# Denominators of two residue parities in one matmul, paired transposes and wider dummy matmuls in a fused attention and FFN kernel

## The chip, the cores and the metric

The kernel runs on one core of a Trainium2 chip. The metric is the device time of one execution in microseconds (us). The median of three runs of the kernel before is 296.57 us (296.5 to 296.87).

The core has five engines with queues of their own: TensorE (PE), VectorE (DVE), ScalarE (ACT), GpSimd (POOL) and SyncE (SP). PE loads one operand into its array (the weights; PEld in the profile) and streams the other past it, one column after another. An operand of at most 64 partitions and 64 columns occupies one quadrant of the 128 by 128 array, and matmuls in different quadrants can run side by side.

## The reference

Eight batches of eight heads with 576 tokens and a head dimension of 64. Heads 0 to 3 attend to the last 32 tokens, heads 4 to 7 to 32 tokens at a distance of four from one another (the dilated heads). The output feeds a two-layer FFN with a squared ReLU.

```python
scores = scale * np.matmul(q, k.transpose(0, 1, 3, 2))
rel = pos[:, None] - pos[None, :]
mask_plain = (rel >= 0) & (rel < 32)
mask_dil = (rel >= 0) & (rel < 32 * 4) & (rel % 4 == 0)
attn = np.exp(scores masked); attn = attn / sum(attn)
x = matmul(attn, v)  ->  [4608, 512]
out = np.maximum(x @ w_in, 0) ** 2 @ w_out        # 512 -> 2048 -> 512
```

## The kernel before, in words

**Layout.** Tokens are taken as m*4 + r: r is the residue (0 to 3), m runs to 144. A dilated head then needs only tokens of the same residue. With r = 2c + j, j is the parity of the residue and c its half. Heads go in pairs e: e = 0, 1 are plain, e = 2, 3 dilated; a pair's two sides lie in partitions 0 to 63 and 64 to 127.

**The order of work.** The kernel schedules itself: each engine runs its instructions in the order in which the program issues them. The FFN is a list of groups of matmuls (`ffn_groups`, lines 967 and 1014, with evictions at 980, 983 and 1020). After group number g come the codes of the g-th part of the string `PROGRAM`, and the steps that a list of due places gives (`natural_step`). Attention for batch 0 is done ahead of the FFN and in its first groups by `first_step`, for batch 1 by `batch1`, for batches 2 to 7 by `quadrants`.

**Dummy matmuls.** At the start, while the first loads are on the way, the code s34x151 runs `turn(34, 151)` (line 760): 34 matmuls of zeros with 151 columns each, into a bank that nobody reads. They begin when the zeros are set. The transposes of batch 0 (line 790) follow on PE as soon as their queries and keys have landed.

**Transposes of batch 1.** The code 1t0 transposes queries and keys of the first 64 residue rows of all heads (line 564), between two FFN groups. The plain heads lie in partitions 0 to 63 of the staging tiles, the dilated ones in partitions 64 to 127. For each operand and each of eight slots z (head pair and residue) there are two transposes of 64 by 64 for the plain pair, to the lower and to the upper half of a PSUM bank, and two for the dilated heads, again to the lower and the upper half. The list is sorted by operand and slot, so that four transposes in four quadrants follow one another. The code 1cq0a and three others copy the results out, on ACT (one) and DVE (three); the scores (1s0) come three groups later. The second part of batch 1 (1t1p, 1t1d) has 80 rows and its own transposes; its dilated ones already take two residues at a time, 80 by 128.

**Denominators.** In `quadrants`, the sums of the exponentials are matmuls against a matrix of ones, issued by `issue` (line 369) as the other quadrant matmuls are. `issue` picks the quadrant whose clock of columns is furthest behind. For a dilated pair, batch 2 sums two pieces of 80 columns for both halves c of one parity (160 columns a matmul); batches 3 to 7 use sums formed before (`shared`) and have pieces of 48, 32 and 48. Each is done for j = 0 and for j = 1. The exponentials of the two parities lie 448 columns apart in the tile `pt`; `turn_` tells that they are stored in the other order. In `batch1`, the code 1b0 does the same for the first part with 128 columns for each parity.

Of the kernel before, what the change touches and what calls it, by code (L numbers as in the profile page):

```python
# [12 lines left out]
RES = 4  # L13
# [6 lines left out]

PROGRAM = (
# [42 lines left out]
def kernel(  # L64
# [10 lines left out]
    P = nc.NUM_PARTITIONS  # L75
    B, H, S, D = q.shape
# [19 lines left out]
    XB = 2  # L96
# [277 lines left out]
    def quadrants(scs, pvs):  # L374
# [16 lines left out]
        for n, (b, e) in enumerate(pvs):  # L391
# [16 lines left out]
            for g, rows in enumerate(sides):  # L408
# [29 lines left out]
                            D_.append((dend if to is None else d4[:, :, to], one, blk(i)[:, :, ms], z))  # L438
                    D_.append((d4[:, :, 112:120], one, blk(7)[:, :, 16:24], 32))
                else:  # L440
                    for j in range(2):
                        y = 448 * (j ^ turn_)
                        both = w[:, y : y + 320].rearrange("p (c m) -> p c m", c=2)
                        for m0, m1, rhs in (
                            (0, 80, both[:, :, 0:80]),
                            (48, 128, both[:, :, 80:160]),
                        ) if b == XB else (
                            (0, 48, both[:, :, 0:48]),
                            (48, 80, shared[rows, e - NE // 2, j ^ turn_]),
                            (80, 128, both[:, :, 112:160]),  # L450
                        ):
                            D_.append((d4[:, j::2, m0:m1], one, rhs, 2 * (m1 - m0)))
                    for x in range(2):
                        ms = slice(48 * x, 48 * x + 80)
                        for j in range(2):
# [68 lines left out]
    def batch1(code: str):  # L524
# [14 lines left out]
        if what == "t":  # L539
            at = code[2:] or "pd"  # L540
            todo = []
            for dil in ([0, 1] if part == 0 else ["pd".index(at[0])]):
                for x, nm in enumerate("qk") if part == 0 or not dil else [("qk".index(at[1]), at[1])]:
                    t = staged(1, nm)
                    if part == 0 and x == 0 or part and not dil or dil and part:
                        pool, name = (ps_f, "pf") if part and not dil else (ps_a, "pa")
                        bank = pool.tile([P, 1024], bf16, name=name)
                    to = bank[:, 512 * x : 512 * x + 512] if part == 0 else bank[:, 0 : 2 * w]
                    two[nm, dil] = to = to.rearrange("p (z m) -> p z m", m=n)
                    for z in range(2 * RES):  # L550
                        if part and dil:
                            todo.append((z, x, to[:, z, :], t[0:n, 1, H // 2 + z // 2, P * (z % 2) : P * (z % 2) + P], 0))
                            continue
                        for hl, rows in enumerate(sides):
                            if not dil:
                                src = t[0:n, part, 2 * (z // RES) + hl, D * (z % RES) : D * (z % RES) + D]
                            else:
                                r = 2 * (z % 2) + hl
                                src = t[64 : 64 + n, 0, H // 2 + z // 2, D * r : D * r + D]
                            todo.append((x, z, to[rows, z, :], src, 64 * (dil and part == 0)))  # L560
            if part == 0:
                todo.sort(key=lambda x: x[:2])
            for _, _, to, src, y in todo:
# [53 lines left out]
        elif what == "b":  # L617
# [6 lines left out]
            for e in (2, 3, 0, 1):  # L624
# [10 lines left out]
                for g, rows in enumerate(sides):  # L635
                    cols, P_, D_ = sides[g ^ crossed(1, e)], [], []
                    one = ones[rows, rows]
                    if e >= NE // 2:
                        for j in range(2):
                            y = 2 * cut * j + cut * (e - NE // 2)  # L640
                            main = two["p"][rows, y : y + cut].rearrange("p (c m) -> p c m", c=2)
                            for blk, _, q0, q1 in far_blocks[part]:
                                to, y0, z = slice(q0 - m0, q1 - m0), 48 * blk, q1 - q0
                                vt = vds[1, 1][rows, e - NE // 2, blk] if part else vds[1][rows, e - NE // 2, 0]
                                for half in range(2):
                                    r = 2 * half + j
                                    P_.append((f"o{e}", o[cols, r, to], vt[:, D * r : D * r + D], main[:, half, y0 : y0 + z], z))
                                d, key = ds[j * part]
                                d = d[cols, :, to] if part else d[cols, j::2, to]
                                D_.append((key, d, one, main[:, :, y0 : y0 + z], 2 * z))  # L650
                    else:
                        y = 0
                        for i, _, q0, q1 in blocks(1, e, part):
                            z = RES * (q1 - q0)
                            to, rhs = slice(q0 - m0, q1 - m0), byr(two["n", e][rows, y : y + z])
                            P_.append((f"o{e}", o[cols, :, to], vbd[1][rows, e, i, rows], rhs, z))
                            D_.append((ds[0][1], ds[0][0][cols, :, to], one, rhs, z))
                            y += z
# [629 lines left out]
```

## Time and profile before

| | |
|---|---|
| median of three runs | 296.57 us |
| the profiled execution | 296.83 us |
| its span, first to last instruction | 294.9 us |
| PE busy | 287.0 us (97%), 3323 matmuls |
| ACT busy | 186.9 us (63%) |
| DVE busy | 155.0 us (53%) |
| POOL busy | 123.6 us (42%) |
| FFN matmuls, line 967 | 127.8 us busy, 697 |
| FFN matmuls, line 1014 | 126.1 us busy, 571 |
| stretch of the transposes 1t0 | 39.71 to 40.43 us |

Matmuls overlap in the array, and the length that a row gives for one reaches to its modelled end; how fast a stream runs is read from one start to the next. A row of the order of time merges instructions of one kind that follow closely: it gives the start of the first, the time to the end of the last, and their count. `64*64` in a PE row is the number of rows and columns of the array that the instruction uses, `64x80` the shape of what it streams. Some matmul records are missing from the trace, which shows as a gap of one matmul's length put down to "issue".

### The profile page before, as it was taken

To read this page: it belongs to the slowest core of one execution; us is meant where nothing else is said; L and a number is where in the kernel's file an instruction comes from. 1 tells how busy PE (TensorE), PEld (TensorE's weight loads), DVE (VectorE), ACT (ScalarE), POOL (GpSimd) and SP (SyncE) were. 2 spreads that over 40 slices of the span, in tenths; PEclk is the share of its full clock that TensorE was granted. 3 is DMA by queue.
4 is the path that set the end of the run, shared out by engine and by line. 5 is a ranking of instruction groups with operands and counts; after the bars stand their busy time and mean duration, and the time that the engine had idled before them with its cause. 6 is when DMAs were issued, how large, how long until landed. Compare 5 with 4: busy or idle time off the path is not lost.

```text
span 294.9 us, 8115 instructions
## 1 busy us (share of the span) xinstructions
PE 287.0 (97%) x3323; PEld 166.3 (56%) x3351; DVE 155.0 (53%) x452; ACT 186.9 (63%) x379; POOL 123.6 (42%) x208
## 2 busy tenths in 40 slices
PE   7899999999999999999999999999999999999995
PEld 6689646859555554555455545554554455445443
DVE  2676225656669656686659464947455244005400
ACT  6788636868767774988567657766776466126511
POOL 8685267676648949376672779000000000000000
PEclk9999999999999999999999999999999999999999
DMA  7999999999999999999999599012101200121022
GB/s 118 192 178 208 206 219 188 173 193 172 178 220 170 125 207 140 190 118 150 154 178 132 79 155 177 7 36 75 36 0 39 73 36 2 36 71 36 2 71 71
DMA packets 82996, 35.48 MB, mean 120 GB/s; under 512 B 52384, under 2 KB 78208, under 8 KB 82960
## 3 DMA queue, kind: packets, MB, share of 16 engines
q0 software_dynamic: 49056, 18.49, 55.7%
q1 hardware_dynamic: 33760, 16.38, 27.6%
q8 instruction: 26, 0.43, 0.6%
q10 hardware_dynamic: 144, 0.10, 0.1%
q14 instruction: 10, 0.08, 0.1%
HBM read 37.50 MB, written 9.44 MB: 159 GB/s over the span
## 4 chain that ended last, share of the span: by engine, by line
PE 93%; DMA 2%; issue 1%; ACT 1%; POOL 1%; DVE 1%; ACTq 0%; POOLq 0%
PE pf L967 42%; PE pf L1014 42%; DMA kb<-in_k_dram 2%; PE po L369 2%; PE pa L369 2%; PE pf L369 2%; PE pd L369 1%; PE pa L790 1%; ACT h2T L980 1%; POOL qb L173 0%; PE pa L564 0%; DVE xT L913 0%; PE pf L842 0%; ACT rec L903 0%; PE po L760 0%
## 5 line engine op out<-in xcount | busy, mean ns | idle before, releaser
L967 PE MATMUL pf<-xT,w_in 128*128 128x512 bf16 (+1 forms) x697 | 127.8, 340 | 0.8 <-DVE xT L913 0.4
L1014 PE MATMUL pf<-w_out_sb,h2T 128*128 128x512 bf16 (+2 forms) x571 | 126.1, 373 | 1.5 <-issue 0.6
L980 ACT ACTIVATE h2T<-pf 128x512 bf16<-128x512 f32 x144 | 84.5, 600 | 32.1 <-PE pf L967 31.8
L967 PEld LDWEIGHTS <-w_in 128*128 128x128 bf16 x704 | 77.9, 113 | 47.0 <-issue 0.6
L983 DVE TENSOR_TENSOR h2T<-h2T 128x512 bf16<-128x512 bf16 x144 | 60.4, 425 | 63.1 <-ACT h2T L980 60.8
L1014 PEld LDWEIGHTS <-h2T 128*128 128x128 bf16 x592 | 56.1, 98 | 63.9 <-issue 0.3
L323 POOL DMA_DIRECT2D vbd<-in_v_dram x80 | 43.5, 554 | 21.7 <-DMA kb<-in_k_dram 9.1
L1020 ACT COPY osb<-pf 128x512 f32<-128x512 f32 (+1 forms) x34 | 19.5, 575 | 52.0 <-PE pf L1014 51.9
L173 POOL DMA_DIRECT2D qb<-in_q_dram x19 | 13.7, 720 | 8.4 <-DMA xx<-qb 6.6
L709 ACT ACTIVATE rec<-rec 128x576 f32<-128x576 f32 x24 | 16.4, 683 | 0.7
L173 POOL DMA_DIRECT2D kb<-in_k_dram x19 | 13.3, 699 | 6.8 <-DMA w_in<-in_moe_w_in_dram 2.9
L195 POOL DMA_DIRECT2D vbd<-in_v_dram x16 | 10.9, 685 | 9.6 <-DMA qb<-in_q_dram 3.9
L726 ACT ACTIVATE pt<-pa 128x384 bf16<-128x384 f32 (+1 forms) x26 | 11.7, 498 | 4.7 <-DVE xT L716 3.8
L309 POOL DMA_DIRECT2D vd<-in_v_dram x20 | 12.2, 621 | 4.5 <-DMA vbd<-in_v_dram 4.5
L315 POOL DMA_DIRECT2D vbd<-in_v_dram x20 | 12.0, 617 | 2.9 <-DMA vbd<-in_v_dram 2.9
L712 DVE TENSOR_TENSOR xT<-pf,rec 128x512 bf16<-128x512 f32 x11 | 7.6, 692 | 10.4 <-ACT rec L709 10.4
L712 DVE TENSOR_TENSOR xT<-po,rec 128x512 bf16<-128x512 f32 x13 | 9.0, 691 | 6.5 <-ACT rec L709 6.3
L728 DVE TENSOR_TENSOR pt<-pt,mask_f 128x384 bf16<-128x384 bf16 x24 | 8.5, 356 | 6.2 <-ACT pt L726 6.1
L728 DVE TENSOR_TENSOR pt<-pt,mask_n 128x384 bf16<-128x384 bf16 (+1 forms) x20 | 7.2, 374 | 8.6 <-ACT pt L726 8.5
L337 DVE COPY qT<-xx 64x576 bf16<-64x576 bf16 (+1 forms) x30 | 10.4, 348 | 0.6
L369 PEld LDWEIGHTS <-vbd 64*64 64x64 bf16 x328 | 8.3, 107 | 4.2 <-issue 3.7
L726 ACT ACTIVATE pt<-pf 128x448 bf16<-128x448 f32 (+1 forms) x18 | 8.6, 519 | 1.0 <-PE pf L369 0.7
(157 smaller groups left out, 281.0 us busy)
## 6 DMA issues: line engine op xcount, KB each, us to landing
qb<-in_q_dram POOLq DMA_DIRECT2D x7, 320.0 KB, 7.7
kb<-in_k_dram POOLq DMA_DIRECT2D x7, 320.0 KB, 9.6
vd<-in_v_dram POOLq DMA_DIRECT2D x34, 64.0 KB, 5.6
w_out_sb<-in_moe_w_out_dram POOLq DMA_DIRECT2D x4, 512.0 KB, 12.2
out_dram<-osb SPq DMA_DIRECT2D x16, 128.0 KB, 5.0
qb<-in_q_dram POOLq DMA_DIRECT2D x6, 256.0 KB, 6.9
kb<-in_k_dram POOLq DMA_DIRECT2D x6, 256.0 KB, 7.9
out_dram<-osb SPq DMA_DIRECT2D x9, 160.0 KB, 3.1
```

What stands on the lines that cost most here:

```text
L173: nc.gpsimd.dma_start(t[p0 : p0 + n, part, h0:h1, :], src[b, h0:h1, t0 : t0 + RES * n, :].rearrange("h (p r) d -> p h (r d)", r=RES),)
L323: nc.gpsimd.dma_start(v_rows[b % 2][p0 + 16 * r : p0 + 16 * r + 16, e, :, :], v[b, 2 * e + hl, :, :].rearrange("(i m r) d -> r m i d", r=R ...
L369: nc.tensor.matmul(out, lhs, rhs, start=begin, stop=True, skip_group_check=True)
L709: nc.scalar.activation(rec[:, :], rec[:, :], ACT.Exp, scale=-1.0)
L712: nc.vector.tensor_tensor(out=tok[:, :, 16:M], in0=byr(o[:, :]), in1=byr(rec[:, 0:512]), op=ALU.mult)
L726: nc.scalar.activation(pt, sp[b, e][g][:, 0:n], ACT.Exp, scale=SCALE)
L728: nc.vector.tensor_tensor(out=pt, in0=pt, in1=mask, op=ALU.mult)
L967: nc.tensor.matmul(to, w_in_sb[piece][:, kt, c0 : c0 + 509 : 4], rhs, start=(kt == kts[0] and x == 0), stop=(kt == kts[-1] and x == per - ...
L980: nc.scalar.activation(hv, acc[u][:, :].rearrange("p (x n) -> p x n", x=per), ACT.Relu)
L983: nc.vector.tensor_tensor(out=hv, in0=hv, in1=hv, op=ALU.mult)
L1014: nc.tensor.matmul(cur[m][:, c0:c1], h2[:, f, P * m : P * m + P], w_out_sb[:, f, c0:c1], start=(f == 0), stop=(f == NF - 1),)
L1020: (nc.vector.tensor_copy if last and part == 1 or tk0 == 3 * NT // 2 else nc.scalar.copy)(osb[:, c0:c1], cur[m][:, c0:c1])
```

## The change

Three edits; nothing moves between engines, and no wait is written by hand. PE has 102 matmuls fewer.

1. The dummy matmuls at the start: 20 of 256 columns in place of 34 of 151.
2. The denominators of a dilated pair: one matmul for both parities, with twice the columns, in `quadrants` (batches 2 to 7) and in the first part of `batch1`. A step of -1 over the parity takes the place of the swapped offset where `turn_` is 1.
3. The dilated transposes of 1t0: one of 64 rows by 128 columns for two residues, in place of two of 64 by 64. The list is sorted as before; in the built order each slot issues two 64 by 64 transposes of the plain pair and then one of 64 by 128.

```diff
-    "... L1:v0dp s34x151 T00 ..."
+    "... L1:v0dp s20x256 T00 ..."
...
-                    for j in range(2):
-                        y = 448 * (j ^ turn_)
-                        both = w[:, y : y + 320].rearrange("p (c m) -> p c m", c=2)
-                        for m0, m1, rhs in (
-                            (0, 80, both[:, :, 0:80]),
-                            (48, 128, both[:, :, 80:160]),
-                        ) if b == XB else (
-                            (0, 48, both[:, :, 0:48]),
-                            (48, 80, shared[rows, e - NE // 2, j ^ turn_]),
-                            (80, 128, both[:, :, 112:160]),
-                        ):
-                            D_.append((d4[:, j::2, m0:m1], one, rhs, 2 * (m1 - m0)))
+                    both = w[:, :].rearrange("p (j y) -> p j y", j=2)[:, :: 1 - 2 * turn_, 0:320]
+                    both = both.rearrange("p j (c m) -> p j c m", c=2)
+                    for m0, m1, rhs in (
+                        (0, 80, both[:, :, :, 0:80]),
+                        (48, 128, both[:, :, :, 80:160]),
+                    ) if b == XB else (
+                        (0, 48, both[:, :, :, 0:48]),
+                        (48, 80, shared[rows, e - NE // 2, :: 1 - 2 * turn_]),
+                        (80, 128, both[:, :, :, 112:160]),
+                    ):
+                        to = d4[:, :, m0:m1].rearrange("p (c j) m -> p j c m", c=2)
+                        D_.append((to, one, rhs, RES * (m1 - m0)))
...
+                        if dil:
+                            todo.append((x, z, to[:, z, :], t[64 : 64 + n, 0, H // 2 + z // 2, P * (z % 2) : P * (z % 2) + P], 64))
+                            continue
                         for hl, rows in enumerate(sides):
-                            if not dil:
-                                src = t[0:n, part, 2 * (z // RES) + hl, D * (z % RES) : D * (z % RES) + D]
-                            else:
-                                r = 2 * (z % 2) + hl
-                                src = t[64 : 64 + n, 0, H // 2 + z // 2, D * r : D * r + D]
-                            todo.append((x, z, to[rows, z, :], src, 64 * (dil and part == 0)))
+                            src = t[0:n, part, 2 * (z // RES) + hl, D * (z % RES) : D * (z % RES) + D]
+                            todo.append((x, z, to[rows, z, :], src, 0))
...
-                                d, key = ds[j * part]
-                                d = d[cols, :, to] if part else d[cols, j::2, to]
-                                D_.append((key, d, one, main[:, :, y0 : y0 + z], 2 * z))
+                                if part:
+                                    d, key = ds[j]
+                                    D_.append((key, d[cols, :, to], one, main[:, :, y0 : y0 + z], 2 * z))
+                        if part == 0:
+                            both = two["p"][rows, 0 : 4 * cut].rearrange("p (j e c m) -> p j e c m", j=2, e=2, c=2)
+                            d = ds[0][0][cols, :, :].rearrange("p (c j) m -> p j c m", c=2)
+                            D_.append((ds[0][1], d, one, both[:, :, e - NE // 2, :, :], 2 * cut))
```

2 rows, old and new, of the table PROGRAM are left out of this document.

## The prediction, made before the result was known

> **What bounds the kernel now.** I read the page first (busy time, slices, chain), then TensorE's waits, then one stretch that holds the whole middle of the run, and at the end the order of time around each line that the diff touches. The page:
>
> ```profile
> span 294.9 us, 8115 instructions
> PE 287.0 (97%) x3323; PEld 166.3 (56%) x3351; DVE 155.0 (53%) x452; ACT 186.9 (63%) x379; POOL 123.6 (42%) x208
> PE 93%; DMA 2%; issue 1%; ACT 1%; POOL 1%; DVE 1%; ACTq 0%; POOLq 0%
> ```
>
> The first line is the span, the second the busy shares, the last the shares of the chain that ended last. TensorE (PE) is busy for 97% and carries 93% of the chain. What it waited for longest over the whole run (us, times, longest), and one window (its length, PE's busy time and matmuls, clock, DMA share, GB/s):
>
> ```profile
> PE po L760 <- DVE kbd L1038: 1.1, 1, 1.1
> PE pa L790 <- DMA kb<-in_k_dram: 1.0, 2, 0.5
> 24.00:290.00 266.00, 264.06 (x2906) 1.00 0.82 117
> ```
>
> Both waits belong to the start: the first dummy matmul, and the first batch's keys. From 24 to 290 us PE lacks 1.9 us of being busy throughout, at the full granted clock. So after the start there is no wait that could swallow extra work: what is added to PE's in-order stream there comes out at the end, one for one, and so does what is taken away.
>
> **The second batch's transposes.** This is the large term. The old stage, in order of time on PE (start, length to the end of the last one, line, output<-inputs, rows*columns of the array in use, moving shape, count):
>
> ```profile
> 39.71 0.45 PE L564 MATMUL pa<-mk,qb 64*64 64x64 bf16 x32
> 39.98 0.51 PE L564 MATMUL pa<-mk,kb 64*64 64x64 bf16 x32
> 40.43 0.39 PE L1014 MATMUL pf<-w_out_sb,h2T 128*128 128x512 bf16 x1
> ```
>
> All 64 have one form, 64*64. Plain heads read partitions 0 to 63, dilated ones 64 to 127, each writing the lower or the upper half of the output, so four run side by side: 32 in the 0.27 us from 39.71 to 39.98, or 0.034 us for a round of four. The stage, from its first start to the next FFN matmul, takes 0.72 us.
>
> The change makes of each two dilated transposes one that fills all 128 columns over 64 rows. The list is still sorted by operand and slot, and in the built order each slot now issues two 64*64 transposes of the plain heads and then one of 64*128, sixteen times. So the array's form changes 31 times inside the stage, where it never changed before. What such a change costs:
>
> ```profile
> 12.41 0.19 PE L896 MATMUL pf<-pt,ones 128*128 128x64 bf16 x1
> 12.53 0.25 PE L880 MATMUL po<-pt,vd 64*64 64x64 bf16 x4
> ...
> 46.79 0.20 PE L564 MATMUL pf<-mk,kb 80*64 80x80 bf16 x1
> 46.92 0.26 PE L369 MATMUL pa<-pt,vd 64*64 64x64 bf16 x8
> ...
> 11.67 0.21 PE L790 MATMUL pa<-mk,kb 80*64 80x80 bf16 x2
> 11.80 0.26 PE L880 MATMUL pf<-pt,vbd 128*128 128x96 bf16 x2
> ...
> 49.34 0.45 PE L564 MATMUL pa<-mk,qb 80*128 80x80 bf16 x8
> 49.62 0.28 PE L967 MATMUL pf<-xT,w_in 128*128 128x256 bf16 x1
> ...
> 10.42 0.20 PE L842 MATMUL pf<-xx 64*64 64x64 bf16 x2
> 10.55 0.39 PE L760 MATMUL po<-kbd 128*128 128x512 bf16 x1
> 10.87 0.22 PE L842 MATMUL pf<-xx 64*64 64x64 bf16 x2
> ...
> 229.50 6.64 PE pf L1014 x30
> ```
>
> In the stage above a 64-column round is followed after 0.03 us. Before a change of form the next matmul starts 0.12 us after one of 64 columns (first pair). The second pair changes only the rows (80 rows need all 128), the third only the columns: 0.13 us each for 80 columns. The fourth shows that the wait is not a matter of leaving transposes: 80*128 needs the same array as 128*128, and eight transposes and the next FFN matmul follow one another every 0.035 us. The next three rows show one matmul alone between two changes, as the stage would have: 0.13 us into it and 0.32 us out of it, against the 0.22 us of a 512-column step (last row, of the chain: 30 in 6.64 us).
>
> So a change costs about 0.09 to 0.10 us over the work, in both directions and for either dimension. The new stage has 32 stretches (16 pairs, whose two run side by side, and 16 singles), each followed by a change, the last by the one to the FFN. At 0.12 us for a stretch that is 3.84 us, at 0.14 (0.13, and the 0.01 more that the lone matmul showed) 4.48; I take the middle, 0.13: 4.16 us, against 0.72 before: 3.4 us more. If a change between two forms with disjoint rows costs nothing, the stage stays at 16 rounds of 0.034 us and about its 0.72: that is the other end, no gain of note, since the two halves were already running side by side.
>
> The pages of the Trainium skill bear on the one thing that no row shows, a change between 64*64 and 64*128. "TensorEngine Tiling (Array Packing)", section Tiling Modes, says that "Changing tiling mode (not just tile) drains the TensorE", and lists these two as different modes; the rows above agree for four other changes, and by that rule the term is the 3.4 us. The same section says that tiles operate independently, which by itself would give the zero.
>
> What stands behind the stage is not late for a second reason:
>
> ```profile
> 40.56 0.59 ACT L569 COPY xx<-pa 128x512 bf16<-128x512 bf16 x1 [0.16 <-PE pa L564]
> 42.12 0.41 DVE L571 COPY qT<-pa 128x512 bf16<-128x512 bf16 x1
> 43.12 0.32 PE L369 MATMUL pa<-xx 64*64 64x64 bf16 x16
> ```
>
> The copies out of the transposes' banks follow them by 0.16 us and end at 42.53; the scores that use them start at 43.12. Copies and scores shift together with PE, so this slack of 0.6 us stays. ACT's and DVE's evictions of later FFN groups are queued behind those copies, but their producers on PE shift as well. No DMA is moved past another; loads issued by POOL become early relative to PE.
>
> **The denominators.** For a dilated pair of batches 3 to 7 each half of the partitions issued 96, 64 and 96 columns twice; it now issues 192, 128 and 192. The columns are the same; what goes is what a matmul costs beside its columns. By group (count, busy us, mean ns, idle before) and in order of time:
>
> ```profile
> L369 PE MATMUL pd<-pt,ones 64*64 64x64 bf16 x28 | 5.2, 193 | 0.0
> L369 PE MATMUL pd<-pt,ones 64*64 64x128 bf16 x22 | 4.5, 218 | 0.0
> 52.94 0.21 PE L369 MATMUL pd<-qT,kbd 64*64 64x96 bf16 x2
> 53.12 0.19 PE L369 MATMUL pd<-qT,kbd 64*64 64x64 bf16 x2
> 47.07 0.28 PE L369 MATMUL pa<-pt,ones 64*64 64x128 bf16 x8
> ```
>
> In the first two rows 64 columns more cost 25 ns, so 0.4 ns each. Four rounds of 96 columns lie between 52.94 and 53.12, so one is 45 ns, of which some 39 are columns. A round of 64 is 34 ns; one of 128 is 60 (eight in two rounds: 0.28 less the 0.22 of one). Merging two of 96 saves about 4 ns, two of 64 about 8: some 15 ns for each pair and half. The halves use different quadrants and run at once, so 5 batches by 2 pairs give 0.15 us. In batch 2 (four 160-column pieces become two of 320) and in the second batch's first part (two of 128 become one of 256) the same 4 ns count five times: 0.02 us, inside the rounding. The ends: nothing, if another quadrant of the visit ends later; and 36 matmuls taken out of a row at a whole 34 ns each, 1.2 us. I take 0.15, since the columns stay. The new reads have one dimension more and for some halves run backwards over the parities; no row has a backward read, and I count it as nothing, from the 96-column rounds above, whose reads and writes are already split (24 by 4) and cost no more than their columns and those few ns.
>
> **The dummy matmuls.** 34 of 151 columns (5134) become 20 of 256 (5120).
>
> ```profile
> 1.07:4.01 2.94, 2.94 (x24) 1.00 0.65 109
> 4.12 0.76 PE L760 MATMUL po<-kbd 128*128 128x151 bf16 x9
> 4.52 0.36 PE L760 MATMUL po<-kbd 128*128 128x151 bf16 x3
> 4.81 0.31 PE L790 MATMUL pa<-mk,qb 64*64 64x64 bf16 x8
> 5.55 0.22 PE L790 MATMUL pa<-mk,kb 64*64 64x64 bf16 x2 [0.43 <-DMA kb<-in_k_dram]
> ```
>
> The first row is a window from the first of them to 4.01 us: 24 in 2.94 us, 0.122 us each. The next two are the last nine and the last three: six of them lie between 4.12 and 4.52, 0.067 each. The array runs at half speed first and at full speed from some 4 us on, which the granted clock does not show. With the same columns the new ones end where the old did. If the full speed came later they would run at 0.207 us each, to 5.2 us, and the first query transposes would still be done at about 5.5, when the keys land at 5.55. The 0.43 us wait for that DMA is the cover; cost 0.
>
> **The sum.** Profiled execution: 296.83 us around its span of 294.9; 3.4 - 0.15 makes it 300.1. It lies 0.26 over the median of the runs shown, 296.57, so the forecast is **299.9 us**, 299.5 to 300.2 by the 0.12 and 0.14 us.
>
> **The rivals.**
>
> *Disjoint rows need no stop* (not slower). The single transpose sits in rows 64 to 127, the pair in rows 0 to 63; if PE stops only where forms overlap, the stage stays at 0.72 us and the denominators' 0.15 remain: 296.4 us. Against it: every change among the rows above stops; for it: in all of them the rows overlap, so they cannot tell. It decides once a change costs under about 0.02 us. 12%.
>
> *Only one direction stops*, say into the wide form: 16 stretches of 0.13 us and 16 of 0.034 are 2.6 us, 1.9 more than before: 298.3 us. The rows show both directions stopping alike. 6%.
>
> *The array falls back to half speed.* For 4.2 us PE would stream 64 columns in every 0.13 us, about a fifth of its time. If that counts as idle, the following FFN runs like the first dummies, at 0.122 instead of 0.067 for a step; a slow stretch as long as that first one, 2.94 us, loses 2.94 x (1 - 0.067/0.122) = 1.3 us: 301.2 us. Against it: at the start PE twice waited 0.5 us for keys between small transposes, and the 512-column matmul at 10.55 us still took full-speed time. 8%. The Trainium skill ("TensorE: Matmul & The Clock Gate", Part 1) puts the fall behind an idle window of about 3.4 us, and its Part 4 has transposes not counting as busy; no run here shows either, and by its own window the loss would be an estimated 1.7 us.
>
> **How the numbers follow.** The forecast's own mechanism has 74%, the rivals 12, 6 and 8. The range is 298.0 to 301.2: it holds the forecast's mechanism, up to 0.17 us for a stretch (4.6 us net of 0.72), and the one-direction case, 80% together; the clock's fall starts at its upper edge. A difference of 0.2% (0.6 us) is about what can be told from no change. The no-stop rival at 296.4 is within it, unless the removed matmuls save toward their upper end: 0.10 for the same, 0.03 for faster. All the rest is slower: 0.87.
>
> **What would show it.** In the changed profile: 48 transposes at the stage's line, 16 of them 64*128, with starts about 0.13 us apart at each change, and the stage 4 us long instead of 0.72; FFN groups behind it shifted by 3.4 us, all else on PE equal but for shifts; visits with dilated denominators 15 ns shorter; the key transposes at the start unmoved at 5.55. If wide and narrow transposes start within 0.03 us of each other the forecast is wrong at its main step; a stage of 4 us with FFN steps of 0.4 us behind it is the clock.

## The result and the profile after

The changed kernel takes 306.98 us (median of six executions, 305.42 to 310.28) against 296.72 for the kernel before on the same chip (six, 296.44 to 299.25): a ratio of 1.0319 with a 95% interval of 1.0257 to 1.0381. It is slower, as forecast, but by 10.3 us where 3.3 were forecast, and lies above the range. The ratios, here and below, leave out executions whose clock was unusually low (here the one of 310.28 us; in a_narrow two, of 303.2 and 303.6), so they differ from the ratio of the medians. The profiled execution took 309.0 us, 12.2 more than the profiled execution of before. Its page (span, busy time, the granted clock in 40 slices, the shares of the chain):

```profile
span 307.1 us, 7911 instructions
PE 294.5 (96%) x3221; PEld 169.1 (55%) x3249; DVE 156.5 (51%) x452; ACT 187.3 (61%) x379; POOL 122.9 (40%) x208
PEclk9999997999799999999999999999999999999999
PE 85%; DMA 9%; POOL 3%; issue 1%; DVE 1%; ACT 0%; ACTq 0%; POOLq 0%
```

PE has 102 matmuls fewer and is busy for 7.5 us more. In two slices (of 7.7 us each) the granted clock is down, and the chain now runs 9% over DMAs, where it ran 2%. The waits of PE, by length (us, times, longest):

```profile
PE pa L369 <- DVE qT L278: 2.8, 1, 2.8
PE pf L845 <- issue: 1.2, 1, 1.2
...
PE pf L970 <- DMA w_in<-in_moe_w_in_dram: 0.7, 1, 0.7
...
PE pa L369 <- DMA xx<-qb: 0.6, 1, 0.6
```

None of these four was there before. The stage of the transposes, in order of time on PE (the first three rows are the stage as a whole; of the others, from narrow stretches inside it, each merges what follows it closely, so only its start and form are read):

```profile
41.33 2.30 PE L563 MATMUL pa<-mk,qb 64*64 64x64 bf16 x24
43.56 2.30 PE L563 MATMUL pa<-mk,kb 64*64 64x64 bf16 x24
45.79 0.61 PE L1017 MATMUL pf<-w_out_sb,h2T 128*128 128x512 bf16 x1
...
41.75 0.35 PE L563 MATMUL pa<-mk,qb 64*128 64x64 bf16 x3
41.88 0.35 PE L563 MATMUL pa<-mk,qb 64*64 64x64 bf16 x3
42.03 0.34 PE L563 MATMUL pa<-mk,qb 64*128 64x64 bf16 x3
```

The stage takes 4.46 us instead of 0.72. A wide transpose is followed after 0.13 us by a narrow pair, and that after 0.15 us by the next wide one: 16 times 0.28 us. Windows over the stage, the stretch behind it and a later one (us; PE busy, weight loads, DVE, ACT, POOL; granted clock, DMA share, GB/s):

```profile
41.33:45.79 4.46, 4.46 (x49) 3.18 (x49) 0.00 (x0) 0.58 (x1) 2.31 (x4) 1.00 1.36 215
45.79:49.20 3.41, 3.19 (x9) 1.21 (x10) 1.35 (x3) 0.58 (x1) 3.18 (x6) 0.50 1.14 145
79.90:83.30 3.40, 3.40 (x18) 2.44 (x17) 1.78 (x6) 2.24 (x6) 1.11 (x2) 0.51 1.57 192
```

Right behind the stage the clock is halved (0.50 of full speed) for 3.41 us, and once more at 79.9.

Both kernels issue the same instructions on ACT in the same order, so how far each of them is shifted says where the 12.2 us arise:

| place in the changed kernel | shift added, us |
|---|---|
| first batch's scores (PE out of instructions, 13.8 to 15.0) | 0.8 |
| up to 24.5 (PE waits for a load of w_in) | 0.9 |
| the stage of the transposes | 3.7 |
| half clock, 45.8 to 49.2 | 1.7 |
| third batch's scores (waits of 0.55 and 2.75) | 3.6 |
| half clock, 79.9 to 83.3 | 1.6 |
| the rest, to the end | -0.1 |

From 84 us on the shift stays at 12.1 to 12.2 us. So the longer stage itself is less than a third of it; the third batch's scores and the half clock behind them are more. Where these come from, the order of time on SP, POOL, DVE and PE shows; first of before:

```profile
51.89 1.43 SPq L254 DMA_TRANSPOSE xx<-kb  x1
56.18 1.25 SPq L254 DMA_TRANSPOSE xx<-qb  x1
...
56.88 0.74 POOL L173 DMA_DIRECT2D qb<-in_q_dram  x1
...
63.59 0.17 DVE L345 COPY kbd<-xx 64x128 bf16<-64x128 bf16 x1
```

and of after:

```profile
58.93 2.00 SPq L254 DMA_TRANSPOSE xx<-kb  x1
65.16 2.55 SPq L254 DMA_TRANSPOSE xx<-qb  x1
...
58.15 0.76 POOL L173 DMA_DIRECT2D qb<-in_q_dram  x1
...
75.58 0.27 DVE L345 COPY kbd<-xx 64x128 bf16<-64x128 bf16 x1 [4.87 <-DMA xx<-qb]
...
77.80 0.46 DVE L278 COPY qT<-pd 128x576 bf16<-128x576 bf16 x1
...
78.67 0.33 PE L369 MATMUL pa<-xx 64*64 64x80 bf16 x14 [2.75 <-DVE qT L278]
```

The third batch's dilated queries and keys reach their places by four transposing loads on SP's queue (line 254). Before, they were issued from 51.89 to 56.18, ahead of POOL's loads of the next queries and keys (line 173, from 56.88), and the last landed 6.4 us after its issue, 1.0 us before DVE came to them at 63.59 and found them there. Now SP's queue is 7 to 9 us later, since ahead of these loads stand stores of FFN results that wait for ACT and so for PE; POOL's queue is only 1.3 us later, at 58.15. The order of the two is turned round. The last transposing load lands 10.4 us after its issue, and DVE waits 4.87 us for it. Of these, 1.9 come from its being issued 9.0 us later where DVE is ready only 7.1 us later (70.71 against 63.59), 4.0 from the longer landing, less the 1.0 us of margin before. The copies queued behind it on DVE (line 278) are late with it, and PE waits 0.55 and 2.75 us.

### The profile page after: what moved, and what is told of

It reads as the page before. It is cut to its first block, busy times and chain, and to the rows that moved or that the text cites. A ratio compares the mean times of both kernels' runs of the same rounds, so it can differ in the third digit from the quotient of the medians.

```text
span 307.1 us, 7911 instructions
## 1 busy us (share of the span) xinstructions
PE 294.5 (96%) x3221; PEld 169.1 (55%) x3249; DVE 156.5 (51%) x452; ACT 187.3 (61%) x379; POOL 122.9 (40%) x208
## 4 chain that ended last, share of the span: by engine, by line
PE 85%; DMA 9%; POOL 3%; issue 1%; DVE 1%; ACT 0%; ACTq 0%; POOLq 0%
PE pf L970 39%; PE pf L1017 39%; DMA w_in<-in_moe_w_in_dram 5%; DMA xx<-qb 3%; PE po L369 2%; PE pa L563 2%; PE pa L369 1%; PE pf L369 1%; PE pd L369 1%; POOL vbd L195 1%; POOL qb L173 1%; POOL kb L173 1%; DVE kbd L348 0%; POOL vd L214 0%; DVE qT L278 0%
## 5 line engine op out<-in xcount | busy, mean ns | idle before, releaser
L970 PE MATMUL pf<-xT,w_in 128*128 128x512 bf16 (+1 forms) x697 | 129.7, 344 | 1.1 <-DMA w_in<-in_moe_w_in_dram 0.7
L1017 PE MATMUL pf<-w_out_sb,h2T 128*128 128x512 bf16 (+2 forms) x571 | 127.5, 376 | 1.7 <-issue 0.9
L173 POOL DMA_DIRECT2D qb<-in_q_dram x19 | 13.5, 713 | 18.2 <-DMA xx<-qb 15.6
L729 ACT ACTIVATE pt<-pa 128x384 bf16<-128x384 f32 (+1 forms) x26 | 11.7, 498 | 8.3 <-PE pa L369 4.5
L309 POOL DMA_DIRECT2D vd<-in_v_dram x20 | 12.2, 626 | 4.2 <-PE pa L369 3.2
L337 DVE COPY qT<-xx 64x576 bf16<-64x576 bf16 (+1 forms) x30 | 10.7, 357 | 0.6
L369 PE MATMUL pa<-xx 64*64 64x80 bf16 (+2 forms) x208 | 6.5, 198 | 3.3 <-DVE qT L278 2.8
## 6 DMA issues: line engine op xcount, KB each, us to landing
w_out_sb<-in_moe_w_out_dram POOLq DMA_DIRECT2D x4, 512.0 KB, 13.8
```

The lines of the kernel that those rows point to most:

```text
L173: nc.gpsimd.dma_start(t[p0 : p0 + n, part, h0:h1, :], src[b, h0:h1, t0 : t0 + RES * n, :].rearrange("h (p r) d -> p h (r d)", r=RES),)
L369: nc.tensor.matmul(out, lhs, rhs, start=begin, stop=True, skip_group_check=True)
L970: nc.tensor.matmul(to, w_in_sb[piece][:, kt, c0 : c0 + 509 : 4], rhs, start=(kt == kts[0] and x == 0), stop=(kt == kts[-1] and x == per - ...
L1017: nc.tensor.matmul(cur[m][:, c0:c1], h2[:, f, P * m : P * m + P], w_out_sb[:, f, c0:c1], start=(f == 0), stop=(f == NF - 1),)
```

## The experiments

After the result, three explanations stood beside the long stage. One: the lower clock follows from a stage that leaves the array thinly used; against it, that transposes as such do not count, or that the fall has nothing to do with the stage. Two: the wait for the transposing loads follows from any delay of PE ahead of them; against it, that the wide transposes themselves or the later clock bring it. Three: the wait at the start comes from the number of instructions in the dummies; against it, from their length.

**The two halves of the change (a_narrow, b_wide_only).** The first is the changed kernel with the old 64 narrow transposes; the second is the kernel before with the wide transposes alone.

```diff
 # a_narrow, against the changed kernel (b_wide_only: the reverse, in the kernel before)
-                        if dil:
-                            todo.append((x, z, to[:, z, :], t[64 : 64 + n, 0, ...], 64))
-                            continue
...
+                            if not dil:
+                                src = t[0:n, part, 2 * (z // RES) + hl, ...]
+                            else:
+                                r = 2 * (z % 2) + hl
+                                src = t[64 : 64 + n, 0, H // 2 + z // 2, D * r : D * r + D]
+                            todo.append((x, z, to[rows, z, :], src, 64 * (dil and part == 0)))
```

> The changed kernel with its transposes of the second batch put back to 64 by 64; dummies and denominators stay changed. Theory (the whole loss comes from the wide transposes and what follows them): 296.4 us, the stage of transposes 0.72 us, no stretch at half clock, visits with dilated denominators about 15 ns shorter. Rival (the dummies let the start run late, as the +0.5 to +1.7 us before the stage in the changed profile suggest, or the denominators' backward reads cost): 297.5 to 298.5 us, with the late first 25 us again in the profile.

> The kernel before with the wide transposes alone. Theory: the same as the changed kernel within its scatter, 305 to 308 us: a stage of 4.4 to 4.5 us, then 3.4 us at half clock, and a later wait for the third batch's scores of about 3 us. Rival (part of the loss belongs to the dummies): 302 to 304 us, without the lateness before the stage.

Measured: 298.8 us for a_narrow (1.0044, interval 1.0 to 1.0088), which is the rival's side, and 304.96 for b_wide_only (1.0283, 1.0238 to 1.0328), just below what was expected. Waits of PE in b_wide_only:

```profile
PE pa L369 <- DVE qT L278: 2.1, 1, 2.1
...
PE pf L841 <- issue: 0.2, 1, 0.2
```

The wide transposes alone bring a stage longer by 3.74 us, half clock for 3.4 us behind it (1.72 us lost) and the wait at the third batch's scores (2.3 us with what hangs on it). The rest of the change brings the wait for instructions at the start, 1.6 us in a_narrow against 0.2 here, and in the profiled execution neither of the other two.

**What the clock follows (c_grouped, f_split, k_dense, s_thin).** c_grouped keeps the wide transposes but does all narrow ones of an operand ahead of its wide ones, so that the form changes three times inside the stage instead of 31.

```diff
-                todo.sort(key=lambda x: x[:2])
+                todo.sort(key=lambda x: (x[0], x[4], x[1]))
```

> The changed kernel with the same wide transposes, sorted so that the plain ones of an operand come first and its eight wide ones after them: 3 changes of form inside the stage instead of 31. Theory (the changes of form cost, not the wide form): 32 rounds of 0.032 us and 4 changes of 0.1 us make a stage of about 1.45 us, 0.75 more than before; no half clock; 297.0 to 297.5 us. Rival (the wide transposes are slow by themselves, or by their weight loads): a stage of 3 us or more and 300 us or more.

Measured: 300.29 us (1.0117, 1.0051 to 1.0183), some 3 us above what was expected. In order of time, its stage:

```profile
40.09 0.78 PE L563 MATMUL pa<-mk,qb 64*64 64x64 bf16 x24
40.79 0.77 PE L563 MATMUL pa<-mk,kb 64*64 64x64 bf16 x24
41.50 1.25 PE L1017 MATMUL pf<-w_out_sb,h2T 128*128 128x512 bf16 x4
```

1.41 us instead of 4.46 with the same 48 transposes: it is the changes of form that cost, as was expected (1.45 us). No half clock follows. The time was missed through waits: 1.4 us for instructions at the start, and the one at the third batch's scores, which stays:

```profile
PE pa L369 <- DVE qT L278: 1.6, 1, 1.6
```

Here the transposing loads are issued only 1.1 to 1.7 us later than before (from 52.94 to 57.88), but POOL's at line 173 begin at 55.84, and the last transposing load landed 11.4 us after its issue. PE also ran out of instructions for 1.0 us at line 272, just ahead of this.

f_split keeps the 31 changes and takes the stage apart: the queries' transposes come two FFN groups earlier, the keys' at the old place.

```diff
-    "M11 | ... |  |  | 1t0 1cq0a 1ck0 1pk0 1pq0 |  |  | 1s0 1e0 1f0 |  | "
+    "M11 | ... | 1t0 |  | 1u0 1cq0a 1ck0 1pk0 1pq0 |  |  | 1s0 1e0 1f0 |  | "
```

> The changed kernel with the queries' half of the wide transposes two FFN groups earlier, so that about 1.7 us of FFN at full rate lies between the two halves; as many changes of form as before. Theory (the clock falls because TensorE streams little for more than a window of about 3.4 us): no stretch at half clock behind the stage, each half 2.2 us, together 3.8 us more than the old stage; 1.7 us better than the changed kernel, 303.5 to 305.5 us, the later wait included. Rival (the clock falls for another reason, the transposes or the changes of form themselves): a stretch at half clock again.

Measured: 307.87 us (1.0354, 1.0302 to 1.0407). Windows over both halves and behind them:

```profile
38.50:45.00 6.50, 6.50 (x53) 3.51 (x51) 0.00 (x0) 1.17 (x2) 4.15 (x7) 1.00 1.36 175
45.00:49.00 4.00, 4.00 (x47) 2.08 (x49) 1.35 (x3) 0.58 (x1) 2.71 (x5) 1.00 1.14 131
```

The two halves together cost 3.8 us, as the stage did, and in the profiled execution no half clock follows either of them: two stretches of 2.2 us with 1.8 us of FFN between them do not bring the fall there. Whether they would in another place is open (see the last section). The total gained nothing all the same, and missed the 303.5 to 305.5 us expected. This kernel had its half clock at 14.8 to 18.2 us instead, behind a wait for instructions at the start, and a wait of 2.5 and 1.4 us at the third batch's scores, with half clock from 76.2 to 83.1.

k_dense issues the 64 narrow transposes six times over in the kernel before, to have as long a stage without a change of form. The repeats write the same results again.

```diff
-            for _, _, to, src, y in todo:
+            for _, _, to, src, y in todo * (6 if part == 0 else 1):
```

> The kernel before with the second batch's 64 narrow transposes issued six times over, densely: a stage of about 3.3 to 3.7 us without changes of form (the first five passes are overwritten by the last, so nothing is left out). Theory (a thin stream lets the clock fall, not the transposes as such): no half clock behind it, 2.6 to 3.0 us more, plus up to 3 us at the third batch's scores. Rival (transposes do not count as work for the clock, however dense): 3.4 us at half clock behind the stage.

Measured: 315.36 us (1.0629, 1.059 to 1.0668). Its waits:

```profile
PE pa L564 <- issue: 8.3, 2, 5.1
```

PE ran out of instructions inside the stage, for 8.3 of its 13.3 us, so the stage was not dense. Half clock came too, but from 44.3 us on, inside the first of these waits. The run does not answer its question.

s_thin answers it from the other side: ahead of the narrow transposes of the kernel before it puts 32 matmuls of zeros with 64 columns, in turn 64*64 and 128*128. There is no transpose among them.

```diff
+            if part == 0:
+                spare = ps_o.tile([P, 512], f32, name="po")
+                for _ in range(16):
+                    for n_ in (64, P):
+                        nc.tensor.matmul(spare[0:n_, 0:64], idle[0:n_, 0:n_], idle[0:n_, 0:64], start=True, stop=True, ...)
```

> The kernel before with 16 pairs of small matmuls of zeros ahead of the second batch's transposes, 64 columns each, one over 64*64 and one over 128*128 in turn: 32 changes of form without a transpose; nothing is left out. Theory (a change costs 0.09 to 0.12 us whatever it stands beside, and a thin stream of 4 us lets the clock fall): a stretch of 4.1 to 4.6 us, then 3.4 us at half clock, then up to 4 us at the third batch's scores: 304 to 307 us. Rival (the clock falls because transposes do not count as work): no half clock behind it, 301 to 304 us.

Measured: 306.06 us (1.0298, 1.0247 to 1.0349). In order of time, and in windows:

```profile
39.00 4.92 PE L567 MATMUL po<-kbd 64*64 64x64 bf16 x32
43.84 0.64 PE L571 MATMUL pa<-mk,qb 64*64 64x64 bf16 x32
```

```profile
39.00:43.84 4.84, 4.84 (x33) 3.33 (x32) 0.00 (x0) 0.59 (x1) 2.53 (x5) 0.82 1.50 236
43.84:48.90 5.06, 5.06 (x75) 2.43 (x75) 1.35 (x3) 0.59 (x1) 3.92 (x7) 0.50 1.34 174
```

The 32 matmuls take 4.84 us, 0.15 each, and the clock falls while they run: a mean of 0.82 is 1.7 us at half. It stays down for 6.8 us in all. So a stream of 64 columns every 0.15 us is enough for the fall, with PE "busy" all the time; that transposes are somehow not counted is not needed for it. That the total lies in the expected range is partly luck: the wait of up to 4 us at the third batch's scores did not come, and in its place PE waited 1.5 us for instructions at 67.6 us and the low clock lasted twice as long as expected.

**A delay that is only a delay (d_delay).** In the kernel before, 25 matmuls of zeros with 512 columns ahead of the transposes: nothing is reordered, the array is full.

```diff
+            if part == 0:
+                spare = ps_o.tile([P, 512], f32, name="po")
+                many = idle[:, :].unsqueeze(1).broadcast_to([P, 2, 256])
+                for _ in range(25):
+                    nc.tensor.matmul(spare[:, :], idle[:, 0:P], many, start=True, stop=True, ...)
```

> The kernel before with 25 matmuls of zeros, 512 columns each, ahead of the second batch's transposes: about 5.4 us of TensorE at full clock in the place where the changed kernel loses 3.7 us in the stage and 1.7 at half clock; nothing is left out. Theory of a shift that grows (a late stage makes the third batch's transposing loads issue later and collide with loads that were not shifted): 304 to 306 us, with a wait of 2 to 3.5 us at the third batch's scores and no half clock before it. Rival (a shift costs itself alone, and the rest of the loss is the clock's): 302.0 us, no wait there.

Measured: 306.55 us (1.0328, 1.0296 to 1.036). Windows over the delay, behind it, and later, with PE's longest wait:

```profile
39.70:45.20 5.50, 5.50 (x27) 2.42 (x25) 0.00 (x0) 0.58 (x1) 3.38 (x6) 1.00 1.49 231
45.20:50.00 4.80, 4.75 (x113) 2.46 (x113) 1.85 (x5) 1.49 (x5) 3.73 (x7) 1.00 1.35 174
77.00:80.40 3.40, 3.40 (x32) 2.44 (x18) 1.07 (x3) 1.78 (x4) 3.10 (x5) 0.50 1.34 128
```

```profile
PE pa L369 <- DVE qT L278: 1.9, 1, 1.9
```

The delay is 5.3 us and the kernel is 9.2 us slower than the kernel before on its chip (297.31), a little more than was expected. In the profiled execution ACT's shift grows by 5.3 us at the delay, 0.8 where PE waits for instructions (0.96 us, at 66.3), 2.1 at the third batch's scores and 1.6 at half clock; with 0.3 ahead of the delay it is 10.0 at the end. Behind the full-width delay there is no half clock. The third batch's scores wait, though no transpose was touched, and half clock comes behind that wait. The last transposing load landed 10.7 us after its issue.

**The loads issued early (e_early).** The changed kernel, with the third batch's transposing loads right behind the second batch's transposes in the program, so that SP issues them before the stores.

```diff
-    ... 1cq0a 1ck0 1pk0 1pq0 |  |  | 1s0 ...  | 1t1dk 1ck1 L2:x0 |  | ... | L2:x1 1f10 | ...
+    ... 1cq0a 1ck0 1pk0 1pq0 L2:x0 L2:x1 |  |  | 1s0 ...  | 1t1dk 1ck1 |  | ... | 1f10 | ...
```

> The changed kernel with the third batch's four transposing loads issued straight behind the second batch's transposes, some 15 us ahead of their old place in SyncE's queue. Theory (the wait for the third batch's scores comes from these loads, which SyncE issues late and which then share the DMA engines with loads that GpSimd had not shifted): that wait is gone, and a second stretch at half clock with it; the stage (3.7 us) and the first half-clock stretch (1.7 us) stay: 302 to 303.5 us. Rival (the scores wait for something else, or the loads are as slow there): 305 us and more.

Measured: 304.39 us (1.0242, 1.0205 to 1.0279). By the medians it is 7.6 us over its own kernel before, where the changed kernel is 10.3 over its own; the time lies between the two expectations. From its trace, taken at a granted clock of 0.95 for most of its length, only order and waits are read. In order of time, the third batch's scores:

```profile
75.35 0.34 PE L369 MATMUL pa<-xx 64*64 64x80 bf16 x16
```

All 16 follow one another with no wait ahead of them. In this execution the second stretch of half clock is gone as well, the one behind the stage is not. But two of the other three executions have a mean clock of 0.988 and 0.989, and 0.989 is what two such stretches left in the changed kernel, so that the second one always goes is not shown. What is left, 7.6 us, is about the rest of the table: 3.7 and 1.7 us, and the start.

**The start (m_filler).** a_narrow with 14 more dummy matmuls of 16 columns: as many instructions as before the change, at almost no length.

```diff
-    "... L1:v0dp s20x256 T00 ..."
+    "... L1:v0dp s20x256 s14x16 T00 ..."
```

> The changed kernel's dummies and denominators with the old transposes, and 14 more dummies of 16 columns behind the 20 of 256, so that TensorE executes as many instructions ahead of the first transposes as the kernel before. Theory (the wait of 1.2 to 1.6 us at the first batch's scores, at 13 to 15 us, is TensorE out of instructions: with 28 fewer of them its next block is fetched later): no such wait, the first 16 KB block of the instruction queue fetched at about 11 us instead of 12.4 to 13.4. Rival (the wider dummies themselves, or the DMA's scatter, cause it): the wait of 1.2 to 1.6 us is there again. Time 296.3 to 297 us by the theory, 297.5 or more by the rival.

Measured: 297.23 us (1.0, 0.9978 to 1.0022), between the two expectations. The first batch's scores, in order of time, of the changed kernel and of m_filler:

```profile
13.47 0.31 PE L845 MATMUL pf<-xx 64*64 64x32 bf16 x9
15.02 0.32 PE L845 MATMUL pf<-xx 64*64 64x32 bf16 x7 [1.23 <-issue]
```

```profile
13.58 0.46 PE L846 MATMUL pf<-xx 64*64 64x32 bf16 x16
```

With the short matmuls PE no longer stops in the middle of the 16. The trace's instruction queue fits this: a first block of 16 KB of instructions is fetched from 10.80 us on in the kernel before and from 11.19 in m_filler, but from 12.70 in the changed kernel and between 12.39 and 13.43 in the five others with 20 dummies and nothing added. Each dummy has a weight load too, so 14 dummies fewer are 28 instructions fewer, and as the fetches stand, PE reaches the place that calls for the block only in the real work; it then waits 1.2 to 1.6 us for it. The number of instructions is the cause, not their length. The Trainium skill ("Runtime: NRT & Kernel Launch", Instruction fetch mechanics) has the same blocks of 16 KiB and calls crossing one "mostly hidden"; here it was not.

**The denominators, and what is worth keeping (n_denom, h_narrow_early, q_denom_early).** n_denom is the kernel before with the new denominators alone. h_narrow_early is a_narrow with the early loads of e_early. q_denom_early is n_denom with the early loads, so with the old dummies and the narrow transposes.

```diff
 # n_denom, against a_narrow
-    "... s20x256 T00 ..."
+    "... s34x151 T00 ..."
 # q_denom_early, against n_denom (h_narrow_early does the same to a_narrow)
-    ... 1pk0 1pq0 |  |  | 1s0 ...  | 1t1dk 1ck1 L2:x0 |  | ... | L2:x1 1f10 | ...
+    ... 1pk0 1pq0 L2:x0 L2:x1 |  |  | 1s0 ...  | 1t1dk 1ck1 |  | ... | 1f10 | ...
```

> The kernel before with the denominators' edit alone. Theory: 0.1 to 0.2 us less on TensorE, no wait at the first batch's scores: a ratio of 0.999 to 1.000. Rival (the backward reads or the other order of the quadrants cost): a visit with dilated denominators longer than before, ratio above 1.001.

> The dummies and denominators of the changed kernel, the old transposes, and the early transposing loads: a candidate to beat both kernels. Theory: 296.0 to 296.6 us, with less scatter than the kernel before, since the third batch's scores have several us of slack. Rival (the loads in their new place delay others that TensorE needs): 297.5 us or more.

> The denominators' edit alone with the third batch's transposing loads issued early: the version that should beat both kernels if any does. Theory: as the denominators alone in its best runs, with fewer late runs, since the third batch's scores have slack: median 296 to 296.6 us, ratio 0.996 to 1.000. Rival (the early loads delay others): ratio above 1.001.

Measured: n_denom 296.68 us (0.999, 0.9968 to 1.0011); h_narrow_early 297.66 (1.0024, 0.9994 to 1.0054), above its 296.0 to 296.6, with a wait of 1.5 us for instructions at the start as in a_narrow; q_denom_early 296.45 (0.9975, 0.9959 to 0.9991). One visit with denominators of a later batch, its first row and the FFN matmul behind it, of before and of n_denom:

```profile
137.59 0.23 PE L369 MATMUL po<-pt,vbd 64*64 64x96 bf16 x2
...
138.78 1.04 PE L1014 MATMUL pf<-w_out_sb,h2T 128*128 128x512 bf16 x3
```

```profile
137.24 0.23 PE L369 MATMUL po<-pt,vbd 64*64 64x96 bf16 x2
...
138.43 1.47 PE L1018 MATMUL pf<-w_out_sb,h2T 128*128 128x512 bf16 x6
```

1.19 us with the old and with the new: the merged matmuls save nothing in this visit. Nor do they over the rest of the run: from 84 us to the end, with all the visits of batches 3 to 7, ACT in n_denom stays 0.33 to 0.43 us ahead of before, and 0.36 at the end. That other quadrants of the visit end last is the likely reason; it was not taken apart. q_denom_early is the only version whose interval lies wholly below 1, by 0.25%. Its best execution, 296.08, is no better than the best of before, 295.98; what it lacks is the scatter (12 executions within 0.9 us, where 29 of before spread over 2.9). The loads alone, without the denominators, were not run, so what part each has is open; since n_denom is level, it is likely the loads.

## Why the prediction was wrong

**The step that failed** is in the first part: "what is added to PE's in-order stream there comes out at the end, one for one". That nothing would swallow the extra time was right. But a delay was not worth itself: 5.3 us of plain delay cost 9.2 (d_delay; 0.8 of it may be the wait for instructions that its own dummies bring), and 3.7 us of wide transposes cost 7.7 (b_wide_only). The prediction had the cause in its hands: "No DMA is moved past another; loads issued by POOL become early relative to PE." The first half holds within each queue and is false between two: SP's transposing loads hang on PE through the stores ahead of them, POOL's in this stretch hardly do (1.3 us later, where SP's are 7 to 9), so a later PE puts the one behind the other. The second half was written down and costed at nothing. Before, no wait shows at those loads, but the trace of before has their landing: the last had 1.0 us of margin. That SP's and POOL's loads lie within a few us of one another could be read there too, against a shift of 3.4 us, and the range had nothing for it.

That issuing them early takes the wait away is shown (e_early). That they land late because POOL's loads are then ahead of them on the same DMA engines is argued, not shown. What speaks for it: where the last of them was issued before POOL's line 173 began, or up to 0.6 us behind (before, a_narrow, m_filler, n_denom), it landed within 7.8 us; where it was issued 2 us behind (c_grouped) or some 6 to 7 (the changed kernel, b_wide_only, d_delay, f_split, k_dense, s_thin), it took 10.0 to 11.7.

**The stage of the transposes**: the mechanism was right and the size nearly. 3.4 us was forecast, 3.74 came: 0.139 us for a stretch, where 0.13 was taken and 0.14 was the upper value. Both directions stop, and disjoint rows spare nothing. The rule of the Trainium skill ("TensorEngine Tiling (Array Packing)", Tiling Modes), that a change of mode drains the array, holds for 64*64 against 64*128 too: 0.13 and 0.15 us from start to start. This is the one thing that no row of before had shown.

**The slack of 0.6 us** behind the stage did stay: the second batch's scores do not wait.

**The dummies**, costed at 0 under the cover of the wait for the keys: that cover held, and the price came elsewhere. The step counted columns and not instructions, and 28 instructions fewer cost 0.8 us at 13.8 (m_filler took this away again). Another 0.9 us goes at 24.5, where PE waits 0.7 us for a load of w_in; why that load is late was not tried and is open. None of the five other traces with 20 dummies and nothing added shows this wait, so it need not come from the change.

**The denominators**, costed at a gain of 0.15: nothing, by the traces of n_denom and of the changed kernel, whose shifts stay level to about 0.1 us from 84 us on. That is the lower end that was named for the case that another quadrant ends last. The backward read over the parities cost nothing that shows either; a gain and a cost of that size that cancel are not excluded.

**The rivals.** No stop between disjoint rows, and one direction only: both fell, by the same two starts. The fall to half speed came: in every one of the changed kernel's executions the mean clock is down (0.978 to 0.994). Behind the stage it lost 1.7 us, where 1.3 was worked out from the first dummies. That it got 8% was the second mistake: it was set up as a case beside the forecast, though it was a consequence of the forecast's own stage of 4 us at a fifth of the array's rate. The row held against it, two waits of 0.5 us at the start, was a ninth as long as what it was to speak for. "TensorE: Matmul & The Clock Gate", Part 1, in the Trainium skill, with its window of about 3.4 us, agrees with the stretches of 3.41 and 3.40 us, and the 1.7 us estimated from it with the loss; its Part 4, on transposes, is not needed, as s_thin shows.

With these the sum goes up from 300.1: 0.3 for the stage, 0.15 for the denominators, 1.7 for the start, 1.7 for the clock, 3.6 for the loads, 1.6 for the second stretch at half clock, and 0.1 off, makes 309.05, against the 309.0 of the profiled execution. The median of the six lies 2 us below the profiled execution; which of the terms are smaller in the others no profile shows, but the mean clock tells a part: the 0.994 of the fastest (305.42) is what one stretch of 3.4 us at half clock would leave, the 0.989 of four, the profiled one among them, what two would.

## What to carry to other kernels

In an array that is used by quadrants, keep instructions of one form together: with 31 changes of form 48 transposes took 4.46 us, with three they took 1.41, and 64 of a single form took 0.72. Before a delay on the bounding engine is counted one for one, look for queues that run on without it, and ask which transfer will then be issued behind which; loads that a later stage needs are worth issuing before the first store that waits on that engine. Cutting instructions at the start of a program also moves when the next ones are fetched, which a count of columns does not show.

## What the runs showed of the hardware that was not expected

- A thin stream halves the clock though PE is busy throughout: 64 columns every 0.13 to 0.15 us for 4.46 us (the changed kernel, b_wide_only, e_early) or 4.84 us (s_thin), with 3.4 us at half behind it, or 6.8 from its last 1.8 us on (s_thin). Two stretches of 2.2 us, 1.8 us apart, did not (f_split), nor one of 1.41 (c_grouped).
- The stretches at half clock keep to a grid. In the clock records of the traces each lasts 3.41 us or a whole multiple of it (those cut off by the end of a run aside), and two in one trace start a whole multiple apart: 45.82 and 79.95 in the changed kernel (10 times 3.41), 14.81 and 76.25 in f_split (18 times). The 3.41 us before the fall were thin throughout in the changed kernel and for 3.06 us in s_thin; of the two steps that f_split's grid gives there, from 38.70 to 42.12 and on to 45.53, the thin halves filled 2.2 and 1.7 us. So f_split shows no fall for its place on the grid and nothing for another place; how much of a step must be thin is not shown.
- PE can run out of instructions. 28 fewer ahead of the first scores cost a wait of 1.2 to 1.6 us there; 384 small transposes in a row cost 8.3 us (k_dense); and waits for instructions of 1.0 to 1.5 us came up in the middle of c_grouped, d_delay and s_thin.
- Transposing loads that landed within 7.8 us of their issue took 10.0 to 11.7 us when they were issued 2 us or more behind the first of another queue's loads.
